# Lightning attention and a snake layer on one core: another written-out order of all operations from group two on

## The chip, the cores and the metric

The kernel runs on one core of a Trainium2 chip. The metric is the device time of one execution in microseconds; the time of the kernel before is the median of four runs. A separate profiled execution gave the trace that all durations below come from.

## What is computed

```python
# q, k, v: (4, 8, 768, 64), lam: (8,);  x: 3072 x 512, w_in: 512 x 2048, w_out: 2048 x 512
for b in range(768 // 64):
    intra = (q_b @ k_b.T * Dmask) @ v_b            # Dmask[i, j] = lam ** (i - j) for i >= j
    inter = (q_b * lam ** (i + 1)) @ kv_state
    out_b = intra + inter
    kv_state = lam ** 64 * kv_state + (k_b * lam ** (63 - i)).T @ v_b
x = out, with the heads of a token side by side
h = x @ w_in
g = h + sin(alpha * h) ** 2 / (alpha + 1e-9)
y = g @ w_out
```

The first part is linear attention with a decaying state, block by block; the second a two-layer network on its result with the snake function between. Inputs and output are float32; the matrix products are taken in bfloat16 with float32 sums.

## The kernel before, in words

**Tiling.** The 3072 tokens are cut into six groups of 512, numbered g = 0 to 5; a group is 256 positions of two batches. The attention of a group is four units, u = 4g to 4g+3 (two batches by two halves of four heads), 24 in all. The state of a batch and half of the heads goes from unit u to unit u+8.

**A unit.** Three loads of 256 KB (`ld.u.0` to `ld.u.2`, q, k and v, line 256) come through rings of eight buffers each. q and k are scaled with powers of lam (`sq`, `sk`, line 297) and v is cast (`cv`, line 281 or 279). q and k are turned so that the head dimension lies on partitions: for units 0 to 7 by TensorE (`tq`, `tk`, copied out by `tcq`, `tck`), from unit 8 on by DMA transposes out of SBUF that SP issues (`tdq`, `tdk`, line 342). TensorE makes the scores (`s`, line 365), VectorE multiplies them with the mask, one half at a time (`m.u.0`, `m.u.1`, line 375), TensorE makes the state's products (`k`, line 401), a copy takes them out (`kc`), GpSimd adds and decays the state (`a`, lines 427 and 431; `n`, line 439). `oi` (line 452) is the product with the state, `o` (line 466) that with the masked scores, and `x` evacuates the sum into the group's transposed activations. The scores have two PSUM banks in all, and `k`, `oi` and `o` of units from 8 on share one place (`okv`), so each waits for the evacuation of the one ahead of it.

**The layer of a group.** `f1.g.f` for f = 0 to 15 are four matmuls of 512 columns each (line 489) into one PSUM bank; in groups 0 and 1 the first four are made in two halves (`f1a` and `f1`). ScalarE takes the sine (`sin`, line 509), ScalarE, GpSimd or VectorE the square (`sqr`, lines 516 and 518), VectorE forms the snake value and so frees the bank (`stt`, line 523). `f2.g.m.j` are four matmuls of the second layer (line 532), for row tile m = 0 to 3 and a quarter j of the sum; `oc.g.m` copies a finished row tile out, and `st.g.m.0` and `st.g.m.1` store its two halves of 128 KB on SP's queue (line 547). The last row tile of the last group is made in two halves of the columns, `lt.0` and `lt.1` (line 555); `ltc.0` and `ltc.1` (last_copy) copy each and issue its two stores at once: both on SP for half 0, one on SP and one on ScalarE's queue for half 1 (line 565).

**Order.** There is no scheduler at build time. A string, ORDER, names each operation with its engine (`T` TensorE, `V` VectorE, `A` ScalarE, `G` GpSimd, `S` SP) and, where it takes a PSUM bank, the bank's number (0 to 3 are h0 to h3, 4 and 5 the two score banks). The loop at line 598 issues them in that order:

```python
    for item in ORDER.split():
        name, eng, *bank = item.split(":")
        kind, *ix = name.split(".")
        ...
        DO[kind](*map(int, ix), eng=ENG[eng], bank=...)
```

An engine executes its own items in the order of the string, one behind the other, and waits for data, buffers and banks by semaphores; items of different engines that stand side by side in the string need not run at one time. SP's queue holds loads, DMA transposes and stores, so a store that waits for its copy holds up the transposes behind it. Items `w.n` are n warm-up matmuls on zeros. `load` (line 252) makes `ld.4.0` wait for the last matmul of f1.0.14 (HOLD), `load_w_in` (line 264) the first weights for a load (GATE).

Of the kernel before, what the change touches and what calls it, by code (L numbers as in the profile page):

```python
# [18 lines left out]
ld.0.0:S ld.0.1:S ld.0.2:S ld.1.0:S tab:V sq.0:V ld.1.1:S ld.1.2:S sk.0:G w.4:T:h2 tq.0:T:2 cv.0:A  # L19
tk.0:T:4 k.0:T:0,1 a.0.0:V sk.1:V ld.2.0:S tcq.0:A tck.0:A w.4:T:s0 s.0:T sq.1:G kc.0.0:A oi.0:T  # L20
tq.1:T:2 tcq.1:A ld.2.1:S ld.2.2:S ld.3.0:S ld.3.1:S wi.0:G ld.3.2:S wi.1:G tk.1:T:0 tck.1:A cv.1:A
m.0.0:V m.0.1:V kc.0.1:V sq.2:V sq.3:G cv.2:G o.0:T x.0.0:A s.1:T tq.2:T:2 sk.2:V m.1.0:V tcq.2:A
m.1.1:V tk.2:T:0 tck.2:A w.3:T:h1 k.1:T:1,2 a.1.0:V sk.3:V s.2:T m.2.0:V kc.1.0:A kc.1.1:A m.2.1:V
oi.1:T tq.3:T:2 tk.3:T:3 tcq.3:A tck.3:A k.2:T:0,1 o.1:T x.1.0:V a.2.0:V w.3:T:s0 s.3:T kc.2.0:A
kc.2.1:A x.1.1:A w.3:T:okv oi.2:T cv.3:G o.2:T x.2.0:A x.2.1:A k.3:T:2,3 kc.3.0:A kc.3.1:A m.3.0:V
m.3.1:V n.0.0:G wi.2:G wi.3:G wo.0:G wo.1:G a.0.1:G a.3.0:V ap:T f1a.0.0:T:1 f1a.0.1:T:5 oi.3:T
o.3:T al:V f1a.0.2:T:0 f1a.0.3:T:4 x.3.0:V x.3.1:A f1.0.0:T sin.0.0:A sqr.0.0:V f1.0.1:T sin.0.1:A
n.0.1:G sqr.0.1:G stt.0.0:V f1.0.2:T n.2.0:G stt.0.1:V wo.2:G a.2.1:G f1.0.3:T sin.0.2:A sin.0.3:A
sqr.0.2:A stt.0.2:V sqr.0.3:A stt.0.3:V f1.0.4:T:3 f1.0.5:T:2 f1.0.6:T:1 sin.0.4:A sin.0.5:A
sqr.0.4:V sqr.0.5:V sin.0.6:A n.2.1:G sqr.0.6:G stt.0.4:V w.3:T:h0 f1.0.7:T:0 sin.0.7:A sqr.0.7:A  # L30
stt.0.5:V stt.0.6:V stt.0.7:V f1.0.8:T:5 sin.0.8:A f1.0.9:T:4 sin.0.9:A sqr.0.8:G sqr.0.9:G
stt.0.8:V stt.0.9:V f1.0.10:T:3 sin.0.10:A sqr.0.10:A stt.0.10:V f1.0.11:T:1 f2.0.0.0:T:2
f1.0.12:T:0 sin.0.11:A sin.0.12:A sqr.0.11:V sqr.0.12:A f1.0.13:T:5 f1.0.14:T:3 sin.0.13:A
stt.0.11:V f2.0.0.1:T f2.0.1.0:T:1 f1.0.15:T:4 f2.0.1.1:T f2.0.1.2:T f2.0.0.2:T ld.4.0:S stt.0.12:V
ld.4.1:S ld.4.2:S ld.5.0:S ld.5.1:S ld.5.2:S ld.6.0:S ld.6.1:S ld.6.2:S ld.7.0:S ld.7.1:S ld.7.2:S
ld.8.0:S ld.8.1:S ld.8.2:S sin.0.14:A sqr.0.13:A ld.9.0:S ld.9.1:S ld.9.2:S stt.0.13:V wo.3:G
n.3.0:G a.3.1:G n.3.1:G sin.0.15:A f2.0.2.0:T:0 n.1.0:G a.1.1:G sqr.0.14:G n.1.1:G stt.0.14:V
sqr.0.15:G sq.4:G sk.4:G stt.0.15:V f2.0.0.3:T sq.5:G sk.5:G oc.0.0:A cv.4:A sq.6:G sk.6:G
f2.0.2.1:T f2.0.1.3:T tq.4:T:5 tk.4:T:3 f2.0.2.2:T tcq.4:V tck.4:V s.4:T k.4:T:2,3 kc.4.0:A kc.4.1:A
cv.5:A oc.0.1:V m.4.0:V a.4.0:V f2.0.2.3:T tq.5:T:4 tk.5:T:3 oi.4:T k.5:T:1,2 m.4.1:V oc.0.2:A o.4:T  # L40
cv.6:G tcq.5:A kc.5.0:A tck.5:V s.5:T tq.6:T:0 n.4.0:G x.4.0:A sq.7:G sk.7:G kc.5.1:V a.5.0:V
tk.6:T:3 f2.0.3.0:T:2 m.5.0:V m.5.1:V tcq.6:A oi.5:T a.4.1:G sq.8:G sk.8:G tck.6:A ld.10.0:S
ld.10.1:S ld.10.2:S k.6:T:1,0 kc.6.0:A kc.6.1:A cv.7:A o.5:T a.6.0:V x.5.0:A s.6:T m.6.0:V m.6.1:V
f2.0.3.1:T tq.7:T:3 tk.7:T:0 oi.6:T o.6:T tcq.7:V k.7:T:1,3 tck.7:A s.7:T f2.0.3.2:T tdq.8:S x.6.0:A
ld.11.0:S a.7.0:V oi.7:T f2.0.3.3:T m.7.0:V m.7.1:V o.7:T x.7.0:V sq.9:G cv.8:A f1a.1.0:T:0 oc.0.3:A
kc.7.0:A f1a.1.1:T:4 f1a.1.2:T:2 f1.1.0:T f1.1.1:T f1.1.2:T k.8:T sin.1.0:A sqr.1.0:V sin.1.1:A
sqr.1.1:V sin.1.2:A sk.9:G stt.1.0:V kc.7.1:V cv.9:G sq.10:G f1a.1.3:T:5 f1.1.3:T f1.1.4:T:1
f1.1.5:T:0 stt.1.1:V ld.11.1:S kc.8:A cv.10:G k.9:T sqr.1.2:G stt.1.2:V kc.9:V sin.1.3:A sqr.1.3:A
sin.1.4:A sin.1.5:A sqr.1.4:A stt.1.3:V sqr.1.5:A tdk.8:S ld.11.2:S f1.1.6:T:3 f1.1.7:T:2 sk.10:G
sk.11:G sin.1.6:A k.10:T kc.10:A a.8.0:G sqr.1.6:A stt.1.4:V tdq.9:S stt.1.5:V sin.1.7:A cv.11:G  # L50
s.8:T n.8.0:G ld.12.0:S ld.12.1:S tdk.9:S sq.11:G f1.1.8:T:1 ld.12.2:S a.9.0:G sq.12:G f1.1.9:T:0
k.11:T sin.1.8:A sqr.1.7:A sin.1.9:A m.8.0:V tdq.10:S ld.13.0:S tdk.10:S tdq.11:S tdk.11:S stt.1.6:V
ld.13.1:S ld.13.2:S f1.1.10:T:3 ld.14.0:S m.8.1:V kc.11:V oi.8:T sin.1.10:A sqr.1.8:A s.9:T o.8:T
tdq.12:S x.8.0:A sk.12:G stt.1.7:V m.9.0:V cv.12:A sqr.1.9:A n.5.0:G a.5.1:G f2.1.0.0:T:2 sqr.1.10:A
n.4.1:G a.10.0:G f2.1.0.1:T stt.1.8:V f1.1.11:T:1 sin.1.11:A m.9.1:V oi.9:T o.9:T x.9.0:A sqr.1.11:A
st.0.0.0:S ld.14.1:S stt.1.9:V stt.1.10:V s.10:T m.10.0:V m.10.1:V a.11.0:G f1.1.12:T:0 f1.1.13:T:3
stt.1.11:V sk.13:G oi.10:T o.10:T sin.1.12:A s.11:T sqr.1.12:V m.11.0:V x.10.0:A f1.1.14:T:1
f2.1.0.2:T tdk.12:S sin.1.13:A m.11.1:V cv.13:A stt.1.12:V oi.11:T o.11:T sqr.1.13:A stt.1.13:V
f1.1.15:T:5 sq.13:G x.11.0:A f1.2.0:T:4 sin.1.14:A sin.1.15:A sqr.1.14:A sqr.1.15:V f1.2.1:T:3
sin.2.0:A sqr.2.0:G sin.2.1:A stt.1.14:V stt.1.15:V sqr.2.1:A stt.2.0:V stt.2.1:V f1.2.2:T:0 sq.14:G  # L60
n.6.0:G f1.2.3:T:1 sin.2.2:A f2.1.0.3:T sk.14:G s.12:T sqr.2.2:A sin.2.3:A sqr.2.3:A k.12:T m.12.0:V
st.0.0.1:S n.9.0:G m.12.1:V f1.2.4:T:3 kc.12:V oc.1.0:V n.7.0:G n.5.1:G tdq.13:S st.0.2.0:S
stt.2.2:V f1.2.5:T:4 stt.2.3:V f1.2.6:T:5 sin.2.4:A sqr.2.4:A sin.2.5:A a.6.1:G stt.2.4:V sqr.2.5:A
n.10.0:G k.13:T kc.13:A f2.1.1.0:T:2 f1.2.7:T:1 sin.2.6:A f1.2.8:T:0 f1.2.9:T:3 f2.1.1.1:T ld.14.2:S
ld.15.0:S ld.15.1:S ld.15.2:S ld.16.0:S sq.15:G tdk.13:S a.13.0:G a.12.0:G sqr.2.6:A cv.14:G oi.12:T
st.0.1.0:S sq.16:G n.12.0:G sin.2.7:A sqr.2.7:A stt.2.5:V stt.2.6:V sin.2.8:A ld.16.1:S ld.16.2:S
ld.17.0:S sin.2.9:A sqr.2.8:A stt.2.7:V stt.2.8:V tdq.14:S n.6.1:G o.12:T a.8.1:G ld.17.1:S tdk.14:S
x.12.0:A sqr.2.9:A s.13:T f1.2.10:T:1 k.14:T kc.14:A m.13.0:V f2.1.1.2:T sk.15:G n.13.0:G a.10.1:G
sk.16:G n.11.0:G m.13.1:V stt.2.9:V oi.13:T f2.1.1.3:T sin.2.10:A o.13:T s.14:T st.0.1.1:S m.14.0:V
oc.1.1:V f1.2.11:T:0 f1.2.12:T:3 st.1.0.0:S tdq.15:S tdk.15:S st.0.2.1:S f2.1.2.0:T:2 f2.1.2.1:T  # L70
st.1.1.0:S f2.1.2.2:T sqr.2.10:A cv.15:A tdq.16:S tdk.16:S a.7.1:G m.14.1:V n.7.1:G x.13.0:A
sin.2.11:A sqr.2.11:A sin.2.12:A cv.16:G a.14.0:G sqr.2.12:A stt.2.10:V stt.2.11:V ld.17.2:S
ld.18.0:S s.15:T ld.18.1:S ld.18.2:S k.15:T sq.17:G f2.1.2.3:T kc.15:A oi.14:T n.14.0:G o.14:T
f1.2.13:T:1 ld.19.0:S st.0.3.0:S stt.2.12:V f1.2.14:T:3 f1.2.15:T:0 m.15.0:V sin.2.13:A sk.17:G
sin.2.14:A a.15.0:G m.15.1:V x.14.0:V oi.15:T oc.1.2:V o.15:T x.15.0:A s.16:T m.16.0:V sin.2.15:A
sqr.2.13:A sqr.2.14:G sqr.2.15:A stt.2.13:V stt.2.14:V stt.2.15:V cv.17:A f2.1.3.0:T:2 f2.1.3.1:T
k.16:T f2.1.3.2:T st.0.3.1:S n.8.1:G m.16.1:V f1.3.0:T:1 sin.3.0:A kc.16:A sq.18:G f2.1.3.3:T
a.11.1:G sqr.3.0:A sq.19:G oc.1.3:V stt.3.0:V f1.3.1:T:4 sin.3.1:A k.17:T f1.3.2:T:3 f1.3.3:T:1
f1.3.4:T:0 sqr.3.1:A sin.3.2:A sqr.3.2:A st.1.0.1:S tdq.17:S stt.3.1:V sk.18:G a.9.1:G n.9.1:G
sin.3.3:A sin.3.4:A sqr.3.3:A sqr.3.4:G stt.3.2:V f1.3.5:T:4 f1.3.6:T:2 f1.3.7:T:5 sin.3.5:A  # L80
sqr.3.5:A sin.3.6:A f1.3.8:T:3 stt.3.3:V stt.3.4:V sin.3.7:A sin.3.8:A sqr.3.6:A stt.3.5:V stt.3.6:V
tdk.17:S ld.19.1:S ld.19.2:S sk.19:G tdq.18:S st.1.2.0:S ld.20.0:S ld.20.1:S ld.20.2:S ld.21.0:S
ld.21.1:S f2.2.0.0:T:0 ld.21.2:S cv.18:G sqr.3.7:G n.10.1:G f1.3.9:T:1 kc.17:A sqr.3.8:A n.11.1:G
stt.3.7:V a.13.1:G stt.3.8:V f2.2.0.1:T k.18:T kc.18:A sin.3.9:A sqr.3.9:A f1.3.10:T:2 sin.3.10:A
sqr.3.10:A a.16.0:G tdk.18:S n.13.1:G sk.20:G stt.3.9:V n.15.0:G tdq.19:S tdk.19:S cv.19:A
f2.2.0.2:T f2.2.0.3:T a.18.0:G oc.2.0:A ld.22.0:S ld.22.1:S ld.22.2:S ld.23.0:S oi.16:T o.16:T
s.17:T f1.3.11:T:3 sin.3.11:A f1.3.12:T:1 f2.2.1.0:T:0 m.17.0:V x.16.0:V m.17.1:V a.12.1:G n.12.1:G
a.17.0:G k.19:T st.1.3.0:S s.18:T m.18.0:V kc.19:A st.1.1.1:S f2.2.1.1:T f2.2.1.2:T f2.2.1.3:T
oi.17:T stt.3.10:V m.18.1:V sq.20:G sq.21:G o.17:T s.19:T oc.2.1:V m.19.0:V m.19.1:V sqr.3.11:A
# [543 lines left out]
```

## Time and profile before

| what | value |
|---|---|
| median of four runs | 220.79 us (219.7 to 221.34) |
| the profiled execution | 221.4 us, of which the span is 219.6 us |
| mean granted TensorE clock | 0.994 |
| TensorE busy | 206.3 us (94% of the span) |
| GpSimd busy | 138.8 us (63%) |
| ScalarE busy | 130.5 us (59%) |
| VectorE busy | 123.5 us (56%) |
| DMA of SP's queue | 29.31 MB, 58.5% of 16 engines' span |
| HBM | 27.28 MB read, 6.29 MB written |

The busy times are sums over the whole span; they overlap each other. A row of groups gives line, engine, operation, output and input with their shapes, the number of instructions, then their busy time together and the mean of one in ns, then the idle time of the engine just ahead of them and what ended it. Matmuls overlap their neighbours, so the mean of one (363 ns for 512 columns) is longer than the distance from one to the next. A row of the timeline gives the start, the time and the engine; PEld is TensorE's loading of weights, SPq and ACTq are issues of DMAs on the queues of SP and ScalarE.

### The profile page before, as it was taken

The numbers are of one execution on the slowest core, as the hardware profiler recorded it, in microseconds if no ns is written. First come the engines' busy times: TensorE is split into PE (matmuls) and PEld (weight loads), VectorE is DVE, ScalarE is ACT, GpSimd is POOL, SyncE is SP. The second block draws the span as 40 slices with busy tenths as digits, with TensorE's granted clock in tenths as the row PEclk, the third lists the DMA queues.
The fourth block names the chain that finished last, engine by engine and source line by source line (L and its number), as shares of the span: only waits on it lengthen the run. The fifth ranks groups of instructions, "written<-read, shape, count | busy, mean of one in ns | idle before, by whom it ended". The sixth has DMA issues, their size and how long they took to land.

```text
span 219.6 us, 5335 instructions
## 1 busy us (share of the span) xinstructions
PE 206.3 (94%) x2068; PEld 109.0 (50%) x2097; DVE 123.5 (56%) x209; ACT 130.5 (59%) x242; POOL 138.8 (63%) x206
## 2 busy tenths in 40 slices
PE   8788999999999999979999999999999999999991
PEld 5556544565645544435444554444544444444460
DVE  3694786286698788565656483357473625613000
ACT  3573986276799799853798636482357447353210
POOL 6387678898899479995939997687471731130000
PEclk9999999999999999999999999999999999999997
DMA  5999999999996979957999737623500004053424
GB/s 134 298 226 192 201 196 200 292 293 291 213 208 154 237 176 243 265 106 189 210 265 225 168 100 168 145 51 71 123 0 3 0 1 96 0 122 67 102 48 96
DMA packets 63849, 33.92 MB, mean 154 GB/s; under 512 B 19648, under 2 KB 60880, under 8 KB 63824
## 3 DMA queue, kind: packets, MB, share of 16 engines
q1 hardware_dynamic: 59488, 29.31, 58.5%
q0 software_dynamic: 4224, 4.19, 12.2%
q8 instruction: 16, 0.26, 0.5%
q10 hardware_dynamic: 112, 0.07, 0.1%
q14 instruction: 9, 0.07, 0.1%
HBM read 27.28 MB, written 6.29 MB: 153 GB/s over the span
## 4 chain that ended last, share of the span: by engine, by line
PE 77%; DMA 5%; POOL 4%; SPq 4%; issue 3%; DVE 3%; ACT 2%; POOLq 0%; ACTq 0%
PE ops L532 33%; PE hps L489 33%; SPq L256 4%; PE okv L466 3%; PE sp L365 2%; DMA QT<-KD 2%; DMA st_k<-in_k_dram 2%; PE okv L452 2%; PE ops L555 2%; PE okv L401 1%; DVE ST L375 1%; POOL QL L297 1%; POOL kvbd L431 1%; POOL kvs L439 1%; PE pt L324 1%
## 5 line engine op out<-in xcount | busy, mean ns | idle before, releaser
L523 DVE SCALAR_TENSOR_TENSOR gall<-s,r_sb,hps 128x512 bf16<-128x512 bf16 x96 | 68.8, 744 | 40.7 <-ACT s L516 25.1
L489 PE MATMUL hps<-xt,w_in_sb 128*128 128x512 bf16 (+1 forms) x403 | 89.4, 363 | 0.8 <-issue 0.2
L532 PE MATMUL ops<-w_out_sb,gall 128*128 128x512 bf16 x352 | 84.8, 379 | 1.4 <-issue 0.9
L509 ACT ACTIVATE s<-hps,alpha_sb 128x512 bf16<-128x512 f32 x96 | 63.4, 685 | 33.8 <-PE hps L489 32.4
L518 POOL TENSOR_TENSOR s<-s 128x512 bf16<-128x512 bf16 x34 | 35.1, 1041 | 43.8 <-ACT s L509 38.5
L489 PEld LDWEIGHTS <-w_in_sb 128*128 128x128 bf16 x416 | 38.8, 98 | 38.9 <-issue 0.2
L532 PEld LDWEIGHTS <-gall 128*128 128x128 bf16 x368 | 34.6, 98 | 39.9
L375 DVE TENSOR_TENSOR ST<-sp,mask 128x512 bf16<-128x512 f32 x48 | 31.6, 685 | 12.5 <-PE sp L365 12.2
L516 ACT ACTIVATE s<-s 128x512 bf16<-128x512 bf16 x54 | 33.3, 630 | 0.7
L297 POOL TENSOR_TENSOR QL<-st_q,E 128x512 bf16<-128x512 f32 x22 | 22.9, 1042 | 2.9 <-DMA st_q<-in_q_dram 2.7
L297 POOL TENSOR_TENSOR KD<-st_k,R 128x512 bf16<-128x512 f32 x21 | 21.8, 1042 | 1.7 <-PE sp L365 1.1
L279 ACT COPY ob<-ops 128x512 f32<-128x512 f32 (+1 forms) x16 | 8.9, 558 | 23.2 <-PE ops L532 17.7
L431 POOL TENSOR_TENSOR kvbd<-kvx,LBD 128x256 bf16<-128x256 f32 x32 | 19.7, 614 | 2.5
L279 ACT CAST xt<-okv 128x512 bf16<-128x512 f32 (+1 forms) x21 | 11.4, 546 | 10.3 <-PE okv L466 8.8
L427 POOL TENSOR_TENSOR kvx<-kva,kvs 128x128 f32<-128x128 f32 x32 | 14.6, 456 | 1.8 <-DVE kva L281 1.6
L365 PE MATMUL sp<-QT 64*64 64x128 bf16 x384 | 10.0, 219 | 1.8 <-DMA QT<-KD 1.4
L466 PE MATMUL okv<-ST,VB 64*64 64x128 bf16 x384 | 10.2, 221 | 0.5 <-DVE ST L375 0.4
L439 POOL TENSOR_TENSOR kvs<-kvx,LHP 128x128 f32<-128x128 f32 x24 | 9.7, 406 | 0.0
L365 PEld LDWEIGHTS <-QT 64*64 64x64 bf16 x384 | 6.8, 106 | 5.1 <-issue 2.3
L279 ACT CAST VB<-st_v 128x512 bf16<-128x512 f32 x13 | 8.0, 619 | 1.3 <-DMA st_v<-in_v_dram 1.3
L452 PEld LDWEIGHTS <-kvbd 128*128 128x128 bf16 x80 | 6.2, 98 | 5.2 <-DVE kvbd L431 0.6
L452 PE MATMUL okv<-QT,kvbd 128*128 128x128 bf16 x80 | 8.4, 219 | 0.2
(60 smaller groups left out, 114.4 us busy)
## 6 DMA issues: line engine op xcount, KB each, us to landing
st_q<-in_q_dram SPq DMA_DIRECT2D x24, 256.0 KB, 4.9
st_k<-in_k_dram SPq DMA_DIRECT2D x24, 256.0 KB, 4.6
st_v<-in_v_dram SPq DMA_DIRECT2D x24, 256.0 KB, 5.2
out_dram<-ob SPq DMA_DIRECT2D x46, 128.0 KB, 2.4
w_in_sb<-in_moe_w_in_dram POOLq DMA_DIRECT2D x4, 512.0 KB, 7.6
w_out_sb<-in_moe_w_out_dram POOLq DMA_DIRECT2D x4, 512.0 KB, 10.2
QT<-QL SPq DMA_TRANSPOSE x16, 3.4
QT<-KD SPq DMA_TRANSPOSE x16, 3.1
```

Source lines behind the costliest of these rows:

```text
L279: nc.scalar.copy(out=out, in_=in_)
L297: eng.tensor_tensor(out=t[:], in0=stage[u, j][:].rearrange("p h two e -> p two h e"), in1=tab[:, :, hh * HH:(hh + 1) * HH].unsqueeze(3).to ...
L365: nc.tensor.matmul(out=sp[hd][half[c], par, hp, :], lhsT=QT[half[hd], 1, par, hp, half[c]], rhs=QT[half[hd], 0, :, hp, half[c]], start=Tru ...
L375: nc.vector.tensor_tensor(out=stm[u][:, hd], in0=sps[u][hd][:], in1=mask[:].unsqueeze(2).to_broadcast([P, 2, 2, P]), op=ALU.mult)
L431: eng.tensor_tensor(out=kvbd[u, c][:], in0=x.unsqueeze(2).to_broadcast([P, 2, 2, D]), in1=LBD[:, 2 * hh:2 * hh + 2, :].unsqueeze(3).to_bro ...
L452: nc.tensor.matmul(out=okv[u][:, c, hp * P:(hp + 1) * P], lhsT=sts[c][:, hp].rearrange("p two e -> p (two e)"), rhs=QT[:, 0, :, hp, half[c ...
L489: f1mm[g, f] = nc.tensor.matmul(out=hps[g, f][:].rearrange("p (b i) -> p b i", b=2)[:, bs] .rearrange("p b i -> p (b i)"), lhsT=w_in_sb[:, ...
L509: nc.scalar.activation(out=s1[g, f][:], in_=hps[g, f][:], func=ACTF.Sin, scale=alpha_sb[:, f:f + 1])
L516: nc.scalar.activation(out=s2[g, f][:], in_=x[:], func=ACTF.Square)
L518: eng.tensor_tensor(out=s2[g, f][:], in0=x[:], in1=x[:], op=ALU.mult)
L523: nc.vector.scalar_tensor_tensor(out=gall[g][:, f, :], in0=s2.pop((g, f))[:], scalar=r_sb[:, f:f + 1], in1=hps.pop((g, f))[:], op0=ALU.mul ...
L532: nc.tensor.matmul(out=ops[g, m][:], lhsT=gall[g][:, f, m * P:(m + 1) * P], rhs=w_out_sb[:, f, :], start=(f == 0), stop=(f == NFC - 1))
```

## The change

ORDER is another one, and nothing else in the file is changed. Both strings hold 1057 items. From group two on the order was searched with two microseconds of slack for every load and every DMA transpose; the attention and the first layer of group zero stand in nearly the same order on each engine as before. The pieces that differ: the places of loads, transposes and stores in SP's queue; the places of the units' operations among the `f1` and `f2` of TensorE; the bank numbers; the engine of some 60 squares, copies and casts (such as `oc.4.2` to `oc.5.1`, which go from ScalarE to VectorE); one warm-up piece of three matmuls (`w.3`), which becomes one of two (`w.2`) at another place; and at the end the stores of the last row tiles, which stand in the order of their tiles, `st.5.2.0` and `st.5.2.1` ahead of `ltc.0`.

The core of the diff, the lines around group one's layer, units 12 to 15, unit 20 and the end:

```diff
--- before.py
+++ after.py
...
-ld.11.0:S a.7.0:V oi.7:T f2.0.3.3:T m.7.0:V m.7.1:V o.7:T x.7.0:V sq.9:G cv.8:A f1a.1.0:T:0 oc.0.3:A
-kc.7.0:A f1a.1.1:T:4 f1a.1.2:T:2 f1.1.0:T f1.1.1:T f1.1.2:T k.8:T sin.1.0:A sqr.1.0:V sin.1.1:A
-sqr.1.1:V sin.1.2:A sk.9:G stt.1.0:V kc.7.1:V cv.9:G sq.10:G f1a.1.3:T:5 f1.1.3:T f1.1.4:T:1
-f1.1.5:T:0 stt.1.1:V ld.11.1:S kc.8:A cv.10:G k.9:T sqr.1.2:G stt.1.2:V kc.9:V sin.1.3:A sqr.1.3:A
-sin.1.4:A sin.1.5:A sqr.1.4:A stt.1.3:V sqr.1.5:A tdk.8:S ld.11.2:S f1.1.6:T:3 f1.1.7:T:2 sk.10:G
-sk.11:G sin.1.6:A k.10:T kc.10:A a.8.0:G sqr.1.6:A stt.1.4:V tdq.9:S stt.1.5:V sin.1.7:A cv.11:G
-s.8:T n.8.0:G ld.12.0:S ld.12.1:S tdk.9:S sq.11:G f1.1.8:T:1 ld.12.2:S a.9.0:G sq.12:G f1.1.9:T:0
-k.11:T sin.1.8:A sqr.1.7:A sin.1.9:A m.8.0:V tdq.10:S ld.13.0:S tdk.10:S tdq.11:S tdk.11:S stt.1.6:V
...
-ld.15.0:S ld.15.1:S ld.15.2:S ld.16.0:S sq.15:G tdk.13:S a.13.0:G a.12.0:G sqr.2.6:A cv.14:G oi.12:T
-st.0.1.0:S sq.16:G n.12.0:G sin.2.7:A sqr.2.7:A stt.2.5:V stt.2.6:V sin.2.8:A ld.16.1:S ld.16.2:S
-ld.17.0:S sin.2.9:A sqr.2.8:A stt.2.7:V stt.2.8:V tdq.14:S n.6.1:G o.12:T a.8.1:G ld.17.1:S tdk.14:S
-x.12.0:A sqr.2.9:A s.13:T f1.2.10:T:1 k.14:T kc.14:A m.13.0:V f2.1.1.2:T sk.15:G n.13.0:G a.10.1:G
-sk.16:G n.11.0:G m.13.1:V stt.2.9:V oi.13:T f2.1.1.3:T sin.2.10:A o.13:T s.14:T st.0.1.1:S m.14.0:V
-oc.1.1:V f1.2.11:T:0 f1.2.12:T:3 st.1.0.0:S tdq.15:S tdk.15:S st.0.2.1:S f2.1.2.0:T:2 f2.1.2.1:T
...
-k.20:T st.1.2.1:S st.2.0.0:S kc.20:A f1.4.0:T:3 sin.4.0:A sqr.3.15:G n.14.1:G tdk.20:S tdq.21:S
...
-st.4.1.1:S f2.4.2.3:T oc.4.2:A st.4.2.0:S st.4.2.1:S f2.4.3.0:T:2 f2.4.3.1:T f2.4.3.2:T f2.4.3.3:T
-oc.4.3:A st.4.3.0:S st.4.3.1:S st.4.0.1:S f2.5.0.0:T:1 f2.5.0.1:T f2.5.0.2:T f2.5.0.3:T f2.5.1.0:T:3
-f2.5.1.1:T f2.5.1.2:T f2.5.1.3:T f2.5.2.0:T:2 f2.5.2.1:T f2.5.2.2:T oc.5.0:A st.5.0.0:S st.5.0.1:S
-oc.5.1:A st.5.1.0:S st.5.1.1:S f2.5.2.3:T lt.0:T:0 oc.5.2:A ltc.0:A lt.1:T:1 st.5.2.0:S ltc.1:A
-st.5.2.1:S
...
+f2.0.3.2:T f2.0.3.3:T m.7.1:V oi.7:T o.7:T n.6.0:G n.4.0:G kc.7.1:V f1a.1.1:T:5 f1a.1.2:T:0 a.6.1:G
+sq.8:G f1a.1.3:T:2 sk.8:G sq.9:G oc.0.3:A x.7.0:A f1.1.0:T f1.1.1:T f1.1.2:T f1.1.3:T f1.1.4:T:3
+sin.1.0:A sin.1.1:A sqr.1.0:V sqr.1.1:V sk.9:G stt.1.0:V sin.1.2:A sqr.1.2:G sin.1.3:A sin.1.4:A
+f1.1.5:T:4 f1.1.6:T:1 stt.1.1:V sqr.1.3:A stt.1.2:V sin.1.5:A stt.1.3:V sq.10:G k.8:T sqr.1.4:G
+sin.1.6:A sqr.1.5:A sqr.1.6:A f1.1.7:T:0 kc.8:V ld.11.0:S f1.1.8:T:5 stt.1.4:V stt.1.5:V stt.1.6:V
+sin.1.7:A cv.9:G k.9:T sin.1.8:A kc.9:V sk.10:G sqr.1.7:A sqr.1.8:A stt.1.7:V stt.1.8:V cv.10:G
+sq.11:G n.3.1:G tdq.8:S tdq.9:S tdk.8:S f1.1.9:T:2 f1.1.10:T:3 f1.1.11:T:1 k.10:T sin.1.9:A
+ld.11.1:S sk.11:G sqr.1.9:A ld.11.2:S tdk.9:S ld.12.0:S kc.10:A sin.1.10:A s.8:T sqr.1.10:A
+f1.1.12:T:0 m.8.0:V a.8.0:G a.9.0:G m.8.1:V oi.8:T sq.12:G tdq.10:S tdk.10:S ld.12.1:S a.4.1:G s.9:T
+o.8:T tdq.11:S tdk.11:S ld.12.2:S stt.1.9:V ld.13.0:S st.0.2.0:S f1.1.13:T:2 sin.1.11:A cv.11:A
...
+sin.2.2:A sqr.2.2:A stt.2.2:V n.4.1:G st.0.1.1:S sk.12:G n.6.1:G f2.1.0.3:T k.12:T n.11.0:G a.5.1:G
+sq.13:G tdq.13:S sq.14:G n.5.1:G f1.2.3:T:4 f1.2.4:T:1 sin.2.3:A sqr.2.3:A f1.2.5:T:0 sin.2.4:A
+sin.2.5:A n.8.1:G tdk.12:S ld.16.2:S cv.13:A st.0.3.0:S kc.12:V f2.1.1.0:T:2 f2.1.1.1:T sqr.2.4:A
+cv.14:A stt.2.3:V f1.2.6:T:4 f2.1.1.2:T f2.1.1.3:T sqr.2.5:A n.9.0:G a.12.0:G stt.2.4:V stt.2.5:V
+sk.13:G sin.2.6:A tdk.13:S k.13:T f1.2.7:T:1 kc.13:V oc.1.0:A f1.2.8:T:0 sqr.2.6:A sin.2.7:A
+sqr.2.7:A oc.1.1:V f2.1.2.0:T:3 stt.2.6:V sk.14:G n.12.0:G s.12:T m.12.0:V sk.15:G sq.15:G k.14:T
+kc.14:A m.12.1:V tdq.14:S sin.2.8:A stt.2.7:V f2.1.2.1:T f2.1.2.2:T oi.12:T a.13.0:G n.7.0:G s.13:T
+o.12:T m.13.0:V a.7.1:G n.7.1:G x.12.0:A m.13.1:V cv.15:G a.9.1:G n.9.1:G st.0.3.1:S f2.1.2.3:T
+f1.2.9:T:1 tdq.15:S tdk.14:S oc.1.2:A oi.13:T o.13:T x.13.0:V f1.2.10:T:3 sk.16:G s.14:T ld.17.0:S
+ld.17.1:S tdk.15:S st.1.0.0:S k.15:T m.14.0:V f2.1.3.0:T:2 f2.1.3.1:T sqr.2.8:G stt.2.8:V a.14.0:G
+sin.2.9:A sqr.2.9:G sin.2.10:A sqr.2.10:A kc.15:A cv.16:G m.14.1:V n.13.0:G sq.16:G a.15.0:G sq.17:G
+stt.2.9:V oi.14:T f1.2.11:T:0 sin.2.11:A sqr.2.11:A s.15:T o.14:T st.1.0.1:S st.1.2.0:S ld.17.2:S
...
+f1.3.13:T:3 sin.3.13:A f2.2.2.0:T:0 oi.17:T st.2.0.0:S a.19.0:G tdq.19:S tdq.20:S st.2.0.1:S
+oc.2.1:A sq.21:G a.13.1:G a.12.1:G sqr.3.12:A f2.2.2.1:T o.17:T stt.3.12:V m.18.0:V x.17.0:A
+tdk.19:S m.18.1:V f1.3.14:T:1 cv.21:G sin.3.14:A sqr.3.13:A sqr.3.14:G f2.2.2.2:T oi.18:T o.18:T
+s.19:T m.19.0:V m.19.1:V f2.2.2.3:T f2.2.3.0:T:2 x.18.0:A stt.3.13:V ld.22.0:S ld.22.1:S oi.19:T
+tdk.20:S s.20:T o.19:T x.19.0:A stt.3.14:V f2.2.3.1:T m.20.0:V f1.3.15:T:3 ld.22.2:S sin.3.15:A
...
+f2.4.2.1:T f2.4.2.2:T f2.4.2.3:T oc.4.2:V stt.5.14:V f2.4.3.0:T:0 st.4.2.0:S stt.5.15:V st.4.2.1:S
+f2.4.3.1:T f2.4.3.2:T f2.4.3.3:T oc.4.3:V f2.5.0.0:T:1 f2.5.0.1:T f2.5.0.2:T f2.5.0.3:T f2.5.1.0:T:5
+f2.5.1.1:T oc.5.0:V st.5.0.0:S st.5.0.1:S f2.5.1.2:T f2.5.1.3:T oc.5.1:V f2.5.2.0:T:4 st.4.3.0:S
+st.4.3.1:S st.5.1.0:S st.5.1.1:S f2.5.2.1:T f2.5.2.2:T f2.5.2.3:T oc.5.2:A lt.0:T:1 st.5.2.0:S
+st.5.2.1:S ltc.0:A lt.1:T:0 ltc.1:A
```

SP's queue, from unit 12's transposes to unit 15's. Before:

```
tdq.12 st.0.0.0 ld.14.1 tdk.12 st.0.0.1 tdq.13 st.0.2.0 ld.14.2 ld.15.0 ld.15.1 ld.15.2 ld.16.0 tdk.13 st.0.1.0
ld.16.1 ld.16.2 ld.17.0 tdq.14 ld.17.1 tdk.14 st.0.1.1 st.1.0.0 tdq.15 tdk.15
```

After:

```
tdq.12 st.0.2.1 ld.15.0 ld.15.1 ld.15.2 ld.16.0 ld.16.1 st.0.1.1 tdq.13 tdk.12 ld.16.2 st.0.3.0 tdk.13 tdq.14
st.0.3.1 tdq.15 tdk.14 ld.17.0 ld.17.1 tdk.15
```

GpSimd's queue after, from the first square of group one to unit 15's scaled q:

```
sqr.1.2 sq.10 sqr.1.4 cv.9 sk.10 cv.10 sq.11 n.3.1 sk.11 a.8.0 a.9.0 sq.12 a.4.1 a.10.0 n.10.0 n.8.0 a.8.1 a.11.0
sqr.1.13 sqr.1.14 n.4.1 sk.12 n.6.1 n.11.0 a.5.1 sq.13 sq.14 n.5.1 n.8.1 n.9.0 a.12.0 sk.13 sk.14 n.12.0 sk.15 sq.15
```

## What the change does to the time: the prediction

> **What bounds the kernel now.** I read five views of the profile before: busy time per slice, the groups, TensorE's waits, the row of time around its one long wait, and the end of the span. The TensorE rows of the first two:
>
> ```profile
> PE   8788999999999999979999999999999999999991
> ...
> PEclk9999999999999999999999999999999999999997
> ...
> L489 PE MATMUL hps<-xt,w_in_sb 128*128 128x512 bf16 (+1 forms) x403 | 89.4, 363 | 0.8 <-issue 0.2
> L532 PE MATMUL ops<-w_out_sb,gall 128*128 128x512 bf16 x352 | 84.8, 379 | 1.4 <-issue 0.9
> ```
>
> TensorE is busy in all slices but the first few, one in the middle and the last, at the full granted clock. "Busy" could still hide half-filled time, so I counted. In the chain of work a step of four 512-column matmuls takes 0.86 us wherever it is repeated, 0.216 us a matmul. Subtracting such steps from the time between them leaves for the small pieces of one unit about 0.35 (k), 0.23 (s), 0.24 (oi) and 0.44 us (o) from group two on. With these, every stretch between 22 us and the last matmul is filled to within 0.2 us, except one, which is 1.4 us too long. TensorE's waits say the same:
>
> ```profile
> engine line waited for: us in total, times, longest us
> PE sp L365 <- DMA QT<-KD: 1.4, 1, 1.4
> PE bz L569 <- DVE warm L190: 1.1, 1, 1.1
> PE ops L532 <- issue: 0.9, 6, 0.2
> ```
>
> The place is s.14, the scores of unit 14:
>
> ```profile
> 92.50 0.42 PE L466 MATMUL okv<-ST,VB 64*64 64x128 bf16 x16
> 94.31 0.42 PE L365 MATMUL sp<-QT 64*64 64x128 bf16 x16 [1.39 <-DMA QT<-KD]
> ```
>
> The end of the span:
>
> ```profile
> 214.80 0.37 ACT L279 COPY ob<-ops 128x256 f32<-128x256 f32 x1 [1.42 <-PE ops L555]
> 215.20 0.56 ACTq L565 DMA_DIRECT2D out_dram<-ob  x1
> 215.25 0.54 SPq L565 DMA_DIRECT2D out_dram<-ob  x1
> 215.83 0.83 SPq L547 DMA_DIRECT2D out_dram<-ob  x1
> ```
>
> The last DMA of the kernel is not the last data: it is st.5.2.1 (L547), whose tile was copied at 211.30. It stands behind last_copy(1) on SP, which waits until 215.25.
>
> **The change part by part.** Both orders do the same work on TensorE, except one warm-up matmul fewer (0.1 us); so what can change is the start, TensorE's waits and the tail.
>
> Start: until the first f1a, which stood at 18.9 us, each engine has the same sequence of operations and SP the same loads; only some banks differ. The start hangs on the arrival of the third k tile at 14.14 (chain of waits: DMA st_k 5.36 us, then VectorE), which no bank touches. I take 0, within 0.3 us either way, no more than the gaps of 0.15 to 0.3 us that TensorE shows there ahead of pieces that wait for a scale.
>
> Tail: SP's last six DMAs were two of last_copy(0), st.5.2.0, one of last_copy(1), st.5.2.1; they become st.5.2.0, st.5.2.1, two of last_copy(0), one of last_copy(1). The two stores are ready at 211.9, cost 0.6 us each on SP and are off it by 213.1, before last_copy(0) wants it at 213.40. The last issue is then the one of 215.25. DMAs of that form land 2.1 us after issue (the row of L565 among the DMA issues; the one on ACT's queue 2.0), at 217.35; st.5.2.1 landed 2.6 us after 215.83, at 218.44. Saved: 1.1 us, with nothing left to hide it. The copies oc.4.2 to oc.5.1 go from ScalarE to VectorE, 0.68 us for 0.58; both are idle there and no matmul waits for them, 0.
>
> The wait of s.14: the DMA transposes tdq.14 and tdk.14 were issued at 86.93 and 88.87, and tdk.14 took 5.39 us to land at 94.27, TensorE having been ready at 92.92. In the changed order 63 steps of 0.86 stand ahead of s.14, before 59; without its own wait it comes at 94.3-1.4+4*0.86, about 96 us. When is tdk.14 issued? It stands behind tdq.15 on SP, which needs the scaled q of unit 15 from GpSimd. GpSimd's queue, from the first square of group one that it takes, sqr.1.2 (f1.1.0 at about 55.9 by the same count of steps, three halves of 0.43, a sine of 0.69 and the signals between: 58.0), holds up to sk.12 ten operations of 1.0 us (back-to-back pitch of scales and squares), two casts of 0.57, six decay pairs of 1.1 and four of 0.36: 19.2, so 77.2 us; up to sq.15 further six of 1.0, two of 1.1 and six of 0.36: 87.5 us. tdq.15 takes 1.2 on SP, tdk.14 is issued at 88.9. The landings of the 32 transposes in the trace reach from 2.4 to 5.9 us: 91.3 to 94.8, before 96. The wait of 1.4 us goes whole.
>
> Here a rule weighs differently. The Trainium skill, "DMA: Bandwidth & Descriptors", Anatomy of one DMA, fits one DMA as 2.0 us plus its bytes by 436 GB/s (measured on DMAs issued from GpSimd): 2.3 us as an estimate for a transpose's 128 KB. By it tdk.14 would have landed at 91.2, TensorE would not have waited, and two microseconds of slack would be bought for nothing: gain 0. The measured 5.39 us decides: transposes here are issued among up to eight others, loads of 256 KB, and the slack has something to cover.
>
> The same sum for the other units, at the worst landing of 5.9 us. The counts of steps ahead of s.u, before and after, are 32/36, 35/37, 38/39, 40/41 for units 8 to 11, 48/58, 56/60, 59/63, 64/66 for 12 to 15, 68/88, 87/90, 90/93, 93/98 for 16 to 19: all later. Only unit 20 is pulled forward, 111 to 100: from 146.9 to about 135. Its tdq.20 needs the buffer that oi.16 reads last, about 122; then on SP tdq.20, st.2.0.1, tdk.19, two loads, tdk.20: 4.2 us, landing at 132.1 at the worst. No wait; TensorE's rows show none that could be gained either.
>
> New waits of compute: I went through each bank that is taken again and each operand, by TensorE's steps between. The shortest distances are of the kinds seen before without a wait (f1 to the same bank again 2.8 us, before 2.76; kv copies 0.86, before 0.86) with one exception: s.8, f1.1.12, oi.8, s.9. Between s.8 and s.9 lie 0.86+0.24 = 1.1 us, and s.9 (and o.8 after it) must wait for both masks of s.8. The nearest row is the first unit of the start: from the end of its scores at 9.67 to the product that needed the masks at 11.05, 1.38 us with VectorE idle. So s.9 waits at least 0.3 us; if VectorE has just begun a snake step (0.66 us pitch), up to 0.9. ScalarE carries much there too: from the first sine of group one to the evacuation of unit 10 14 sines at 0.57, eight squares at 0.525 and five copies make 14.5 us, where TensorE has about 16. I take 0.4; below zero is excluded, as TensorE has no wait to lose there.
>
> Sum: 0 (start) - 1.4 (s.14) + 0.4 (s.9) - 1.1 (tail) = -2.1 us. Span 219.6 to 217.5; the profiled execution took 221.4, 1.8 outside its span, so 219.3, a ratio of 0.9905. The four runs have median 220.79; by the same ratio 218.7 us.
>
> A second rule would turn the sum around: the Trainium skill, "TensorE: Matmul & The Clock Gate", Back-to-back issue gap, gives streams of weight load and matmul 131 ns at 512 columns. Then 0.216 us a matmul would mean that TensorE is held up everywhere, some 60 us (estimate: 720 matmuls by 0.085) could come from feeding it better, and 2 us would be a small part of what an order can do. No row supports it: 0.86 us per four returns in every stage, whatever the other engines do. I keep 0.216.
>
> **The rivals.** (1) The stretch from 57 to 75 us is the new bottleneck. For it: ScalarE was busy 16.35 of 18 us from 60 to 78 before, and the changed order puts seven f1 blocks in a row ahead of k.8. Then waits at s.9, o.9, s.11 and the last units add 0.9+0.3+0.2, the 1.4 are given back and the tail alone is left: 219.7. Against it: the pitches above leave 1.5 us. (2) The change does not do what it says: tdq.15 ahead of tdk.14 waits for GpSimd longer than worked out, and s.14 waits 1 us as before: 219.7 with the smaller part of the rest. (3) Slower: transposes stuck on SP. Before, tdk.18, issued right behind six loads, held SP for 3.0 us instead of 1.2 and landed after 5.9. If every transpose did so, s.14 and s.15 would wait 0.7 and 1.4, s.18 0.4, s.20 1.1, and the queue would push some of it into units 21 to 23; the loads behind come later by as much. It decides from 3.6 us of such waits (2.5 are gained, 1.1 is the bound); at 4.5 it gives 222. Against it: only 3 of 32 held SP over 2 us.
>
> **How the numbers follow.** About 0.5%, 1.1 us, is what a measurement of this kernel can tell from no change. Main case 0.68, 218.0 to 219.5 (s.9 from 0.3 to 0.9, start 0.3, the runs' own scatter); rival 1 0.14, rival 2 0.10, rival 3 0.08. Faster by over 0.5%, under 219.7: most of the main case and half of rivals 1 and 2, 0.74; within 0.18; slower 0.08. The range reaches into rivals 1 and 2, to 220.6, and down to 217.8 for no wait at s.9.
>
> **What would show it.** No wait of TensorE for QT<-KD or QT<-QL over 0.3 us; a wait of 0.3 to 0.9 us for VectorE's ST at about 67 us; 0.86 us steps otherwise; f1a at 18.9; the last DMA a last_copy (L565) issued within 0.5 us of the last copy, and about 3.7 us from TensorE's last matmul to the end of the span instead of 4.9. Wrong would be shown by waits for ACT xt or kva between 60 and 76, or for DMA at s.14, s.15 or s.20.

## The result, and the profile after

The changed kernel takes 219.83 us in the median of 44 runs (219.44 to 220.71), the one before 221.63 us in 63 runs beside it (219.46 to 222.95): a ratio of 0.9937, with an interval of 0.9923 to 0.9951. Ratios here leave disturbed runs out, so they can differ a little from the quotient of two medians (0.9919 here). The profiled execution took 219.62 us with a span of 217.8 us, where that of before took 221.4 and 219.6. The forecast was a ratio of 0.9905: 218.7 us beside the four runs' 220.79, which would be 219.5 beside 221.63. So the direction is right, and the gain is smaller: 1.8 of 2.1 us in the spans, 0.63% of 0.95% in the ratios, where the forecast lies outside the interval. The 219.83 us lie above the main case (218.0 to 219.5) and inside the whole range; 0.8 us of the distance to 218.7 come from the four runs, whose median of 220.79 is lower than that of the 63. Something else changed that no forecast was made of: the runs of before spread over 3.5 us, those after over 1.3, while the fastest of each are equal (219.46 and 219.44). What is gained is gained in the slower executions.

The page of the kernel after, TensorE's slices, its clock, and its two largest groups:

```profile
PE   8788999989999999999999999999999999999992
...
PEclk9999999999999999999999999999999999999999
...
L489 PE MATMUL hps<-xt,w_in_sb 128*128 128x512 bf16 (+1 forms) x401 | 89.0, 362 | 1.1 <-issue 0.5
L532 PE MATMUL ops<-w_out_sb,gall 128*128 128x512 bf16 x353 | 84.6, 379 | 1.4 <-issue 0.9
```

The slice of 7 in the middle is gone, and the groups take what they took. TensorE's waits after, in us in total, times, longest:

```profile
PE bz L569 <- DVE warm L190: 1.1, 1, 1.1
PE ops L532 <- issue: 0.9, 6, 0.2
...
PE kvp L401 <- ACT VB L279: 0.4, 1, 0.4
PE sp L365 <- ACT QT L279: 0.4, 1, 0.4
...
PE okv L452 <- DVE kvbd L431: 0.3, 1, 0.3
PE okv L452 <- POOL kvbd L431: 0.3, 1, 0.3
```

The wait for QT<-KD, 1.4 us before, is no longer in the list. All four lines of the last two blocks are new. Those of kvp and of sp for ScalarE, and the one of okv for GpSimd's kvbd, are where part of the gain went; okv's wait for VectorE's kvbd lies in the start, at 13.88, ahead of the first f1a, which is no later than before. The forecast had looked for a wait for VectorE's ST at about 67 us, and there is none: the two waits of that name in the list stand at 9.85 and 10.45. The tail, ScalarE's and SP's rows at the end of the timeline after:

```profile
212.26 0.37 ACT L279 COPY ob<-ops 128x256 f32<-128x256 f32 x1 [1.16 <-PE ops L555]
212.66 2.21 SPq L565 DMA_DIRECT2D out_dram<-ob  x3
214.01 0.37 ACT L279 COPY ob<-ops 128x256 f32<-128x256 f32 x1 [1.37 <-PE ops L555]
214.41 0.55 ACTq L565 DMA_DIRECT2D out_dram<-ob  x1
```

No L547 stands behind the last copy any more: the last issues are those of last_copy(1). From TensorE's last matmul (213.97) to the end are 3.83 us; they were 4.88.

From the starts of the items in the two traces, after less before:

| part | forecast, us | measured, us |
|---|---|---|
| start, up to the first f1a (18.92 to 18.77) | 0 | -0.15 |
| k.5 and s.5 in group one | 0 | +0.80 |
| s.14's wait | -1.4 | -1.39 |
| s.9 and o.8 | +0.4 | +0.41 |
| everything else on TensorE | 0 | -0.41 |
| tail | -1.1 | -1.05 |
| sum | -2.1 | -1.79 |

Of the -0.41, 0.26 us lie between f2.0.3.0 and s.7 in that one execution of before (4.19 us there, 3.93 in two other executions of it); the rest I did not place.

### The profile page after: what moved, and what is told of

Its sections match the earlier page's. It is cut to its first block, busy times and chain, and to the rows that moved or that the text cites. A ratio compares the mean times of both kernels' runs of the same rounds, so it can differ in the third digit from the quotient of the medians.

```text
span 217.8 us, 5327 instructions
## 1 busy us (share of the span) xinstructions
PE 205.3 (94%) x2066; PEld 107.8 (49%) x2096; DVE 125.1 (57%) x212; ACT 128.7 (59%) x238; POOL 139.4 (64%) x207
## 3 DMA queue, kind: packets, MB, share of 16 engines
q0 software_dynamic: 4224, 4.19, 12.1%
## 4 chain that ended last, share of the span: by engine, by line
PE 77%; POOL 5%; issue 4%; DVE 4%; SPq 3%; DMA 2%; ACT 2%; POOLq 0%; ACTq 0%
PE ops L532 35%; PE hps L489 31%; SPq L256 3%; PE sp L365 3%; DMA st_k<-in_k_dram 2%; PE okv L466 2%; PE okv L452 2%; PE ops L555 2%; POOL KD L297 1%; DVE gall L523 1%; PE okv L401 1%; POOL QL L297 1%; POOL s L518 1%; DVE ST L375 1%; DVE kvbd L431 1%
## 5 line engine op out<-in xcount | busy, mean ns | idle before, releaser
L516 ACT ACTIVATE s<-s 128x512 bf16<-128x512 bf16 x56 | 34.6, 633 | 1.4 <-DVE gall L523 0.5
L279 ACT COPY ob<-ops 128x512 f32<-128x512 f32 (+1 forms) x15 | 8.3, 556 | 26.7 <-PE ops L532 24.1
L279 ACT CAST xt<-okv 128x512 bf16<-128x512 f32 (+1 forms) x20 | 10.8, 546 | 11.0 <-PE okv L466 9.5
L281 DVE COPY ob<-ops 128x512 f32<-128x512 f32 x10 | 6.9, 689 | 13.6 <-PE ops L532 13.6
```

What stands on the lines that cost most here:

```text
L279: nc.scalar.copy(out=out, in_=in_)
L516: nc.scalar.activation(out=s2[g, f][:], in_=x[:], func=ACTF.Square)
```

## The experiments

My theory after the result: the tail and the wait at s.14 give what the forecast says, and the 0.8 us at k.5 and s.5, which the forecast does not have, come from the order of two names in the string. The rivals: that the gain is not these two pieces but the order as a whole, and that the 0.8 us come from something else in group one. In brackets stands the median of the kernel before in the same session.

**The tail alone**, in the kernel before:

```diff
-... lt.0:T:0 oc.5.2:A ltc.0:A lt.1:T:1 st.5.2.0:S ltc.1:A st.5.2.1:S
+... lt.0:T:0 oc.5.2:A st.5.2.0:S st.5.2.1:S ltc.0:A lt.1:T:1 ltc.1:A
```

> The order before with one edit: st.5.2.0 and st.5.2.1 stand right behind oc.5.2, ahead of last_copy(0), as in the changed order. Theory: the last DMA is then last_copy(1)'s of 64 KB, issued 0.6 us earlier and landing 2.1 instead of 2.6 us after its issue; from TensorE's last matmul to the end of the span 3.8 us instead of 4.9, span and time 1.0 to 1.1 us shorter (ratio 0.995). Rival: the landing of the last store is not what ends the span, and the tail is worth under 0.4 us.

Measured: 220.58 us (221.3), ratio 0.9975 (0.9939 to 1.0011). The span of the profiled execution is 218.6, 1.0 us under that of before, and s.14 still waits 1.4 us. The traces give the tail its 1.0 us as a piece by itself; the interval of the times, which spread over 3.4 us, reaches to no change.

**The wait at s.14 alone**, in the kernel before:

```diff
-... ld.16.1:S ld.16.2:S ld.17.0:S ... tdq.14:S ... ld.17.1:S tdk.14:S
+... tdq.14:S tdk.14:S ld.16.1:S ld.16.2:S ld.17.0:S ... ld.17.1:S
```

> The order before with one edit: on SP tdq.14 and tdk.14 stand ahead of ld.16.1 instead of behind ld.17.0 and ld.17.1. Theory: tdk.14 is issued near 86.5 instead of 88.9 us and lands by 92, ahead of TensorE at 92.9; the wait of 1.4 us at s.14 is gone, and as the time before scatters from 219.5 to 223 us because such landings vary, the scatter shrinks too; mean 1.2 to 1.6 us shorter (ratio 0.994). Rival: the wait of the profiled execution is an accident of that one; over many runs the edit is worth under 0.4 us, or the loads of unit 16 and 17, now 2.4 us later, take its place.

Measured: 223.02 us (221.3), ratio 1.0071 (1.0034 to 1.0109): slower. tdk.14 was issued at 86.93 and landed 2.5 us later, and s.14 does not wait. TensorE around it:

```profile
93.14 0.39 PE L365 MATMUL sp<-QT 64*64 64x128 bf16 x16
93.46 1.90 PE L489 MATMUL hps<-xt,w_in_sb 128*128 128x512 bf16 x8
96.72 2.53 PE L532 MATMUL ops<-w_out_sb,gall 128*128 128x512 bf16 x11 [1.36 <-DVE ob L281]
```

VectorE in the same stretch:

```profile
95.98 0.69 DVE L281 COPY ob<-ops 128x512 f32<-128x512 f32 x1 [1.72 <-DMA out_dram<-ob]
```

In the place of the first wait stands one of 1.36 us, eight matmuls further on. f2.1.2.0 waits for its bank, the bank for the copy oc.1.1 on VectorE, and oc.1.1 for an output buffer that st.0.1.1 is still writing out. That store was issued at 90.46 and landed after 5.5 us, at 95.95. VectorE in the kernel before:

```profile
94.77 0.69 DVE L375 TENSOR_TENSOR ST<-sp,mask 128x512 bf16<-128x512 f32 x1 [2.98 <-PE sp L365]
95.38 0.68 DVE L281 COPY ob<-ops 128x512 f32<-128x512 f32 x1
```

There the copy stands behind the mask of unit 14, which waits for s.14, and the store has landed by then, at 94.4. So part of the second wait lay beside the first and did not show: with s.14 early, oc.1.1 could begin at about 94.2. But only a small part. In five executions of the old queue st.0.1.1 landed 3.8 to 4.3 us after its issue, which here would be 94.3 to 94.8, at most 0.6 us too late for the copy and 0.2 for TensorE (estimates from these rows). The rest of the 1.36 us comes from the store's landing after 5.5 us, with the four loads now directly ahead of it. So far as one execution shows, the edit itself made most of the new wait.

The trace does not show the whole loss. Its execution took 221.69 us, 1.3 less than the median of its runs, and its span, 219.9, is only 0.3 us over that of before. That the store is what costs the others more is tested in the next run, by its place.

**Both of these waits**, the store right behind its other half as well:

```diff
-... st.0.1.0:S ... ld.16.1:S ld.16.2:S ld.17.0:S ... tdq.14:S ... ld.17.1:S tdk.14:S ... st.0.1.1:S
+... st.0.1.0:S st.0.1.1:S ... tdq.14:S tdk.14:S ld.16.1:S ld.16.2:S ld.17.0:S ... ld.17.1:S
```

> The order before with the two transposes of unit 14 ahead of ld.16.1 (as in the run that came out slower) and, in addition, st.0.1.1 right behind st.0.1.0 instead of behind tdk.14. Theory: that run lost the gain because st.0.1.1, whose output buffer oc.1.1 needs, landed at 96.0 us behind the loads; VectorE waited with the copy and f2.1.2.0 with it, 1.4 us or more. With the store at about 85 us both waits are gone: 1.4 us or more below the order before (ratio 0.992), no wait of TensorE over 0.3 us after 22 us, and runs within 1.5 us of each other, where those before scatter over 4. Rival: the queue of SP is simply too full there and another load, store or transpose takes the place: no faster than before.

Measured: 220.37 us (221.1), ratio 0.9978 (0.9948 to 1.0009). TensorE in its profiled execution:

```profile
92.74 0.39 PE L365 MATMUL sp<-QT 64*64 64x128 bf16 x16
93.07 1.90 PE L489 MATMUL hps<-xt,w_in_sb 128*128 128x512 bf16 x8
94.81 2.75 PE L532 MATMUL ops<-w_out_sb,gall 128*128 128x512 bf16 x12
```

Neither wait is left, and the span is 218.0, 1.6 us under before. That is what was expected of one execution. Without the store's move the ratio was 1.0071, so the store's place does account for that loss. But the gain over before is only 0.7 us, the interval leaves out the expected 1.4 and reaches to no change, and the runs spread over 2.3 us instead of 1.5: the rival, that something else takes the place, is not ruled out for the other executions. The profiled one, at 219.8 us, is 0.6 under the median of its runs, and that of before, at 221.4, is 0.3 over 221.1.

**Both waits and the tail**, the three edits together:

> The same with the two stores of the last full row tile ahead of last_copy(0) as well. Theory: a further 1.0 us, 2.4 or more below the order before (ratio 0.988, near 218.8 us): all that the changed order gains comes from three places in SP's queue, and without its new waits (0.9 at k.5 and s.5, 0.4 near s.9) these are worth more than the whole new order. Rival: the new order has a merit of its own elsewhere and stays at least as fast.

Measured: 219.47 us (221.1), ratio 0.9938 (0.9913 to 0.9963), span 217.3; eight of the twelve runs took 219.1 to 219.55, four 220.1 to 220.28. The ratio is that of the whole change. So moving five items in SP's queue gives as much as the whole new order, but not more, as the theory had it: 1.6 us in the median, where 2.4 were expected. The spans give 2.3 us, from one execution of before that is slower than the median (221.4 beside 221.1) and from the fastest of these twelve (219.1 beside 219.47). The rival, that the new order stays at least as fast, stands; without its own new wait, in the next run, it is the faster of the two by its ratio, if not clear of the intervals.

**kc.4 named ahead of a.4.0**, in the kernel after; each engine's own sequence stays the same:

```diff
-... f2.0.2.3:T a.4.0:V m.4.1:V ld.5.2:S ld.6.0:S kc.4.0:A kc.4.1:A ...
+... f2.0.2.3:T kc.4.0:A kc.4.1:A a.4.0:V m.4.1:V ld.5.2:S ld.6.0:S ...
```

> The changed order with one edit: the state copies kc.4.0 and kc.4.1 stand ahead of a.4.0 in the string, as before; each engine's own order stays the same. Theory: two readers of one PSUM bank on two engines are ordered by the string, so in the changed order ScalarE's kc.4.0 waits until VectorE's a.4.0 is done (45.8 us instead of 45.0), and with it cv.5 and tcq.5, for which k.5 and s.5 wait 0.45 and 0.43 us; without it both waits are gone: 0.8 us shorter (ratio 0.996 to the changed order, span about 217.0). Rival: cv.5 and tcq.5 are late because the loads of unit 5 or GpSimd's scales are: no change, and the waits stay.

Measured: 219.15 us (221.3), ratio to before 0.9914 (0.988 to 0.9947), span 217.0, 0.8 us under the kernel after. ScalarE in the kernel before:

```profile
45.01 0.43 ACT L279 COPY kva<-kvp 128x128 f32<-128x128 f32 x2 [2.44 <-PE kvp L401]
```

In the kernel after:

```profile
45.83 0.43 ACT L279 COPY kva<-kvp 128x128 f32<-128x128 f32 x2 [3.34 <-DVE kvbd L431]
46.15 0.63 ACT L279 CAST VB<-st_v 128x512 bf16<-128x512 f32 x1
```

ScalarE with kc.4 named first:

```profile
44.94 0.43 ACT L279 COPY kva<-kvp 128x128 f32<-128x128 f32 x2 [2.44 <-PE kvp L401]
45.26 0.63 ACT L279 CAST VB<-st_v 128x512 bf16<-128x512 f32 x1
```

kc.4.0 (ScalarE) and a.4.0 (VectorE) both read the bank that k.4 wrote; neither writes it. The program still lets the one named second wait for the first. After the change that is ScalarE, which waits for VectorE's kvbd instead of TensorE's kvp: 0.9 us later, and with it the cast cv.5 and the copy tcq.5 behind it. TensorE in the kernel after pays for them:

```profile
46.11 0.28 PE L452 MATMUL okv<-QT,kvbd 128*128 128x128 bf16 x2
46.83 0.32 PE L401 MATMUL kvp<-VB,KD 64*64 64x64 bf16 x16 [0.45 <-ACT VB L279]
46.96 0.41 PE L466 MATMUL okv<-ST,VB 64*64 64x128 bf16 x16
47.80 0.42 PE L365 MATMUL sp<-QT 64*64 64x128 bf16 x16 [0.43 <-ACT QT L279]
```

k.5 waits for cv.5, s.5 for tcq.5. With kc.4 named first neither wait exists: s.5 starts at 47.01, f2.0.3.0 at 47.81 instead of 48.61, and s.14 at 96.46 instead of 97.25. The trace shows the 0.8 us. The times by themselves do not yet: the interval overlaps that of the kernel after (0.9923 to 0.9951). But the four kernels here that name kc.4 first have ratios of 0.9907 to 0.9917.

**The reverse, in the kernel before**: its kc.4 and cv.5 named behind a.4.0.

```diff
-... k.4:T:2,3 kc.4.0:A kc.4.1:A cv.5:A oc.0.1:V m.4.0:V a.4.0:V f2.0.2.3:T ...
+... k.4:T:2,3 oc.0.1:V m.4.0:V a.4.0:V kc.4.0:A kc.4.1:A cv.5:A f2.0.2.3:T ...
```

> The order before with kc.4.0, kc.4.1 and cv.5 named behind a.4.0 in the string; each engine's own order is unchanged. Theory: as in the changed order ScalarE's copy then waits for VectorE's a.4.0, k.5 and s.5 wait 0.4 us each, 0.8 us longer in the stretch from 44 to 49 us, though the later wait of s.14 may take some of it back: 0.3 to 0.8 us slower than before. Rival: the loss there belongs to other differences of the changed order: no change, and no wait at k.5 and s.5.

Measured: 221.43 us (221.1), ratio 1.0026 (0.9995 to 1.0056); in its profiled execution ScalarE's kc.4.0, and TensorE's tk.5 and s.5:

```profile
46.21 0.43 ACT L279 COPY kva<-kvp 128x128 f32<-128x128 f32 x2 [3.34 <-DVE kvbd L431]
...
46.70 0.38 PE L324 MATMUL pt<-iden,KD 128*128 128x128 bf16 x4 [0.27 <-POOL KD L297]
...
48.19 0.42 PE L365 MATMUL sp<-QT 64*64 64x128 bf16 x16 [0.43 <-ACT QT L279]
```

ScalarE's wait for VectorE's kvbd appears in the old order too, and s.5 waits for the same copy, so this belongs to the two names and not to the rest of the new order. From s.4 to s.5 it takes 3.49 us, 2.67 before (44.40 to 47.07): the expected 0.8 us. Only one of the two expected waits shows. In this execution tk.5, ahead of k.5, waits for GpSimd's KD, so that cv.5 is done in time; both delays lie beside each other, and s.5 starts when tcq.5 lets it. In the times the edit is not shown: the interval includes no change. The span, 220.7, is 1.1 us over before, and holds 0.3 us more of waiting at s.14 (1.7 us) and a beginning that is 0.3 us late already at s.4.

**a.8.0 ahead of sq.11 on GpSimd**, on top of kc.4 first:

```diff
-sq.11:G n.3.1:G ... sk.11:G ... m.8.0:V a.8.0:G a.9.0:G ...
+a.8.0:G sq.11:G n.3.1:G ... sk.11:G ... m.8.0:V a.9.0:G ...
```

> The changed order with the edit of the copies of unit 4 and a second one: GpSimd's a.8.0 stands ahead of sq.11 instead of behind sk.11. Theory: the 0.25 us that oi.8 waits for GpSimd's kvbd goes (a.8.0 is done 2.4 us earlier); of the 0.4 us lost around s.9 about half stays, as s.9 then waits for the masks of s.8. 0.15 to 0.4 us shorter than with the first edit alone; sk.11 is 1.1 us later, and s.11 has 3.7 us to spare. Rival: the masks alone set s.9, and nothing is gained.

Measured: 219.13 us (221.3), ratio 0.9912 (0.9881 to 0.9943), the same as with kc.4 first alone; the span, 217.5, is 0.5 us longer than there. The question was what delays s.9. VectorE and TensorE in the kernel after, where 0.24 us belong to oi.8 and s.9 should start at 67.70:

```profile
66.70 1.29 DVE L375 TENSOR_TENSOR ST<-sp,mask 128x512 bf16<-128x512 f32 x2 [0.53 <-PE sp L365]
...
67.46 0.22 PE L452 MATMUL okv<-QT,kvbd 128*128 128x128 bf16 x1
67.93 0.34 PE L452 MATMUL okv<-QT,kvbd 128*128 128x128 bf16 x3 [0.25 <-POOL kvbd L431]
68.20 0.42 PE L365 MATMUL sp<-QT 64*64 64x128 bf16 x16
```

With a.8.0 early:

```profile
66.26 1.29 DVE L375 TENSOR_TENSOR ST<-sp,mask 128x512 bf16<-128x512 f32 x2 [0.53 <-PE sp L365]
...
67.02 0.39 PE L452 MATMUL okv<-QT,kvbd 128*128 128x128 bf16 x4
67.34 0.68 PE L365 MATMUL sp<-QT 64*64 64x128 bf16 x16
67.80 0.44 PE L466 MATMUL okv<-ST,VB 64*64 64x128 bf16 x16
```

In the kernel after the second matmul of oi.8 starts 0.47 us behind the first, where 0.06 is the distance of its neighbours, and the masks of unit 8 are done at 67.99, ahead of s.9 at 68.20: the whole 0.41 us is the wait for GpSimd's kvbd, and the masks cost nothing. With a.8.0 early that wait is gone, and s.9 itself takes 0.68 us instead of 0.42. The row names no releaser for the pause inside it, but the masks are done at 67.55, and the first matmul of s.9 into the second score bank starts at 67.60. From the start of oi.8 to the next f1 it takes 1.23 us, 1.32 in the kernel after, where 0.24 + 0.23 + 0.44 = 0.91 would do. So only 0.1 us was to be had; two causes stand in parallel here as well, and with one taken away the other sets nearly the same price.

**The store late, in the new order** (kc.4 first as well): does the kernel after live from st.0.1.1 being early?

```diff
-... stt.2.2:V n.4.1:G st.0.1.1:S sk.12:G ... tdq.15:S tdk.14:S oc.1.2:A ...
+... stt.2.2:V n.4.1:G sk.12:G ... tdq.15:S tdk.14:S st.0.1.1:S oc.1.2:A ...
```

> The changed order with the copies of unit 4 first, and st.0.1.1 moved on SP behind tdk.14 (issued near 93 instead of 83.5 us). Theory: oc.1.1 on VectorE then cannot write its buffer until about 97 instead of 88.6, and everything behind it on VectorE, snake steps and masks, stands still: TensorE loses 5 to 8 us between 90 and 100 us. Rival: VectorE is not on TensorE's path there and the loss is under 2 us.

Measured: 218.89 us (221.1), ratio 0.9917 (0.9892 to 0.9943), span 217.1. My theory fell: nothing was lost. st.0.1.1 landed at 96.64, but oc.1.1 ran at 87.89 and waited for no store. The new order stores group zero's row tiles in another sequence, so another buffer comes free first; which one oc.1.1 takes I inferred from the string and did not see in the trace.

**The kernel before, twice more**, unchanged, for a second and third profiled execution:

> The kernel before, unchanged, for a second profiled execution. Theory: what moves from execution to execution is the landing of tdk.14 and of the DMAs around it; the wait at s.14 is between 0.5 and 3 us and its difference from 1.39 us is the difference of the span from 219.6 us; no other wait of TensorE over 0.4 us after 22 us. Rival: the scatter comes from elsewhere (the start, other transposes), and s.14 waits 1.4 us again.

> The same, a third profiled execution; the same expectations.

Measured: 221.42 us with a span of 219.6, and 220.67 us with 218.9. Scores that wait in the second execution:

```profile
66.55 0.42 PE L365 MATMUL sp<-QT 64*64 64x128 bf16 x16 [0.49 <-DMA QT<-KD]
...
94.34 0.42 PE L365 MATMUL sp<-QT 64*64 64x128 bf16 x16 [1.09 <-DMA QT<-KD]
```

The wait at s.14 is there in every profiled execution of the old queue (1.1, 1.1, 1.4, 1.4 and 1.7 us), and tdk.14 landed after 4.9 to 5.4 us in all five. So this wait belongs to the order and is no accident of one execution. In the second execution s.9 waits too, for tdk.9, which took 5.1 us to land (4.0 to 4.8 in the other four): the theory had no other wait over 0.4 us. This is what the single profile of before could not show: a transpose that is just in time in one execution is late in another.

**All together**: kc.4 first, a.8.0 early and the store late.

> The changed order with the copies of unit 4 first, st.0.1.1 behind tdk.14 (so tdk.14 0.7 us earlier) and a.8.0 ahead of sq.11. Theory: the three are independent, and each of the two last was worth 0 to 0.3 us alone: 218.7 to 219.1 us, ratio 0.990 to the order before. Rival: they share their gain, and it is the 218.9 of the run without a.8.0.

Measured: 218.97 us (221.35), ratio 0.9907 (0.9877 to 0.9936), no better than kc.4 first alone within the intervals. In its profiled execution (span 217.9) the scores of unit 15 wait:

```profile
100.66 0.42 PE L365 MATMUL sp<-QT 64*64 64x128 bf16 x16 [0.65 <-DMA QT<-KD]
```

With st.0.1.1 among the transposes, tdk.15 was issued at 97.27 and landed at 100.6. The slack at one unit had been spent for a store. The version to keep is the kernel after with kc.4 named first, at 0.9914 of the time before (0.988 to 0.9947); the change as it was made stands at 0.9937.

## Why the prediction was right in its parts, and the step that failed

The step that failed is the sum of new waits of compute: it put the pieces of group one at nothing, and k.5 and s.5 cost 0.80 us there. The other large terms, the wait of s.14 and the tail, came out to within 0.05 us.

**Bound and unit cost: right.** Steps of four matmuls stay at 0.86 us, and the mean of a matmul hardly moves (363 to 362 ns, 379 to 379). Nothing of the 60 us (estimate) that the 131 ns of the Trainium skill ("TensorE: Matmul & The Clock Gate", Back-to-back issue gap) would leave to be had was found by another order.

**Start: right.** f1a comes at 18.77, and three profiled executions of the kernel before have it at 18.92, 18.96 and 18.77: the 0.15 us are scatter.

**Tail: right**, -1.05 for -1.1 in the whole change, and 1.0 in the span of the tail alone. The copies moved to VectorE show no wait.

**s.14: right in its sum, not in its reasons.** The wait went whole. But tdk.14 was issued at 92.84, not 88.9. SP in the kernel after:

```profile
88.28 1.22 SPq L342 DMA_TRANSPOSE QT<-KD  x1
89.59 1.22 SPq L342 DMA_TRANSPOSE QT<-QL  x1
90.86 0.58 SPq L547 DMA_DIRECT2D out_dram<-ob  x1
91.55 1.24 SPq L342 DMA_TRANSPOSE QT<-QL  x1
92.84 1.26 SPq L342 DMA_TRANSPOSE QT<-KD  x1
```

I let tdk.14 wait for GpSimd's sq.15 alone and left out that tdk.13, tdq.14, a store and tdq.15 stand ahead of it on SP, 1.2 us each for the transposes. These set the time: SP issues one behind the other here, and tdq.15 went at 91.55, 2.3 us after its sq.15 was done (at 89.3, not 87.5: GpSimd was late as well, but tdq.15 did not wait for it). tdk.14 landed after 4.2 us, at 97.0; s.14 began at 97.25. The slack was 0.2 us where I counted at least 1.2. Rival 2 had the place right, by another cause than its own, and came within 0.2 us of a wait; that there was none is in part luck. The Trainium skill's 2.0 us plus bytes by 436 GB/s ("DMA: Bandwidth & Descriptors", Anatomy of one DMA; 2.3 us as an estimate) would have put the landing at 95.1 with two to spare; the measured 4.2 decides.

What I also missed is that the 1.4 us depend on how the wait is removed: moving the two transposes ahead of four loads left st.0.1.1 directly behind these, oc.1.1 waited for it, and the kernel became slower. In the new order oc.1.1 waits for no store, which the prediction had not looked at.

**s.9: right in place, and in size by luck** (+0.41 for +0.4). I had the masks of s.8 cost it. In the kernel after it is GpSimd's a.8.0, for which oi.8 waits, that costs the 0.41; I had not seen it. The masks cost 0.32 (1.23 - 0.91) once a.8.0 is early, so the reckoning was sound for a cause that stood behind another.

**New waits of compute: here the sum failed.** "The shortest distances are of the kinds seen before without a wait ... with one exception" counted TensorE's steps between uses of a bank. It missed two readers of one bank on two engines: naming kc.4.0 behind a.4.0 cost 0.9 us on ScalarE and 0.8 us on TensorE. Without it the kernel has a span of 217.0 and a ratio of 0.9914, beside a forecast of 217.5 and 0.9905. That is the mis-sized term: +0.8 counted as 0, hidden in part by the 0.4 us of small gains. The operands of k.5 and s.5 come from ScalarE, and what ScalarE's copies themselves wait for was not followed back.

**Rivals 1 and 3: not seen.** No wait for ACT xt or kva between 60 and 76 us, and no transpose that makes the scores wait, in the profiled execution. The queue did lengthen, as rival 3 had it; it stayed inside the slack.

**What stays open.** The old queue with its two known waits and its tail mended (the three edits together) should have gained 2.6 us by the spans of its parts, and gained 2.3 in its own and 0.6% in the ratio. The second execution of before and the last experiment show what can happen in other executions, waits at s.9 and s.15 that come and go, but no slower execution of the three edits was profiled. Nor was one of the transposes moved alone, where the median lies 1.3 us over the profiled execution. That the slack at every transpose is what narrows the runs from 3.5 to 1.3 us fits this and was not tested by itself; the three edits of the queue, without that slack elsewhere, narrow them to 1.2 in twelve runs.

## What to carry to other kernels

Before a wait on a queue is costed as a gain, look at what the move puts behind: the landing of a store frees a buffer, the buffer a copy, the copy a bank, and such a chain shows only when the store is late. In an order written by hand, compare not only each engine's sequence but also the order in which two engines are named for one tile, readers too. Follow an operand back past the engine that delivers it. And where DMAs set the waits, take several profiled executions, and say where each stands among the runs: one that is faster than its median hides what the others lose.

## What the hardware showed that I had not expected

How long a DMA takes to land went here with its place in the queue more than with the execution. tdk.14 landed after 4.9 to 5.4 us in the five executions of the old queue, after 2.45 to 2.47 in the three where it stands ahead of the loads, and after 2.5 to 4.2 in the five of the new order and its variants. st.0.1.1, 128 KB, landed after 3.8 to 4.3 us in the old queue, after 5.5 when the four loads stood directly ahead of it, and after 2.35 in the last experiment. And two engines that only read one PSUM bank ran one behind the other in the order of the program, here 0.9 us apart; that is how the program's waits have it, and no run here took them away.
